# Attention and a feed-forward layer in one kernel: the first batch and the first feed-forward tile put in a written order on all engines

## The chip, the cores and the metric

The kernel runs on one core of a Trainium2 chip. The metric is the time of one execution on the device in microseconds. Before the change it is 1029.81 us, the median of three runs (1029.01 to 1031.52).

## What is computed

For 8 batches of 576 tokens and 8 heads of 64, two attentions in a row, and then a mixing and a feed-forward layer (512 wide, 2048 inside). From the reference, cut:

```python
p_packed = sm_attn(p, k, v)            # 32 packed queries per head
out = sm_attn(q, p_packed, p_packed)   # 576 queries on the 32 packed rows
...
X = np.fft.fft(np.fft.fft(x, axis=1), axis=2)
u = x + np.real(X)
un = (u - mu) / np.sqrt(var + 1e-06)   # mean and variance of each token's 512
ch = np.maximum(un @ w_ch1, 0.0) @ w_ch2
return u + ch
```

## The kernel before

Two kinds of work alternate. `front(b)` (line 241) makes the rows `u` of one batch: attention, the spectrum over tokens and features as products with tables of sines and cosines, the sum with the input and each row's statistics. `ffn` (line 628) takes a tile of 512 rows, four blocks of 128, through the feed-forward layer: 16 rounds of `up` (12 products into `ph`, one PSUM buffer) and `down` (12 products into four accumulators `acc`). There are 8 batches and 9 tiles; a batch gives four blocks, and two batches share one block for the remaining tokens. While `ffn` of tile t runs, `front(t + 1)` is carried on in pieces, one at each of the 31 half rounds (`step`, line 735). "Settled" tiles, 1 to 6, are those with a whole `front` beside them and no weights to load.

All products are made of float32 values split in two parts of fewer bits, the high part by a cast on ACT and the low part by a subtraction on DVE or POOL (`split`, line 98): `hh` and `hl` of the hidden layer, `uh` and `ul` of the rows, `wr_h` and `wr_l` of the weights (`wsplits`, line 618, low part on POOL). The next `up` writes `ph`, and so waits until `hh` (ACT, line 653) and `hl` (DVE, line 654) have read it.

The weights come as 64-bit numbers, 32 pieces of 512 KB. A piece goes by a DMA on SP's queue to a staging place (`fetch`, line 158), ACT takes the high words (`Prelu`, line 179), and DVE shifts them and puts the low bits in (lines 180 and 181). This is done during the first batch and tile 0. The first six pieces are staged in parts of the weight tiles that are filled last (`STG0`), the others in three rotating buffers: one in `ubuf`, two named `wst`.

In `front`, the parts are named by letters in `ORDER` (line 39): s scores, t their transposes, p the packed rows (`packed`, with `bd`, `bdh`, `bdl` for their block diagonal), d the parts of these, q the query scores, g the spectrum of the packed rows (`gh`, `gl`), e, m and a the second softmax in three stages (lines 376 to 428), f, r and h the folding of the weights over tokens (`eo`, `f`, `xl`, `ol`, `fh`, `fl`). 0 and 1 are the two head groups; capitals S, X and U do both groups together; y is a place where the next half round may start. Then follow the products `py`, `pz` and `px`, and `u`. The tables of `py` to `px` are loaded as float32 and split on ACT and DVE (`load_base`, `load_tables`). Between the engines, DVE and POOL share the elementwise work by small tables (`EN`, `EF`, `ES`).

What sets the order: from tile 1 on PE, DVE, ACT and POOL run their instructions as the program writes them (`manual_schedule`, line 748). The first batch and tile 0, with batch 1's `front` beside it, are ordered by the framework's scheduler, which may take a later instruction first; batch 0 and batch 1 have `ORDER` rows of their own. SP's queue always issues in its own order.

Of the kernel before, what the change touches and what calls it, by code (L numbers as in the profile page):

```python
# [16 lines left out]
P = 128  # L17
S = 576
HS = S // 2
D = 64  # L20
# [11 lines left out]
ES = (1, 0, 0)  # L32
# [14 lines left out]
STG0 = [-2, -2, -4, -4, -6, -6]  # L47
STG1 = [9, None, None]
LEAD = 2
# [28 lines left out]
def tile_kernel(ctx, tc, kpT, qT, v, w1, w2, tabC, tabS, tabR, tabB, tabT, sel, ident_d, out):  # L78
# [45 lines left out]
    def load_base():  # L124
        nc.sync.dma_start(sels, sel)
        st = load(tabB, [P, 2, N2], "st_base", "wst")
        h = work.tile([P, 2, N2], F32R, tag="tmp", name="base_h", bufs=3)
        nc.scalar.copy(h, st)
        nc.vector.scalar_tensor_tensor(basis, h.bitcast(F32), selC, st, ALU.mult, ALU.add)
        nc.sync.dma_start(turn, tabT)  # L130

    def load_tables():
        for t, d in enumerate((tabC, tabS)):
            st = load(d, [P, 1, KT], "st_tab", (t, 2))
            split(tbh[t], tbl[t], st[:, 0, :])
        st = work.tile([P, 2, 320], F32, tag="wst", name="st_tabr", bufs=2)
        nc.sync.dma_start(st[:101], tabR)
        for t in range(2):

            h = work.tile([P, DM], F32R, tag="tmp", name="tabr_h", bufs=3)  # L140
            nc.scalar.copy(h[:101, :320], st[:101, t, :])
            nc.vector.scalar_tensor_tensor(
                tbr[t][:101], h[:101, :320].bitcast(F32), selA[:101], st[:101, t, :], ALU.mult, ALU.add)

    sels = cpool.tile([P, 3], F32, name="sels")
    selA, selB, selC = (sels[:, i:i + 1] for i in range(3))
# [9 lines left out]
    def fetch(j, n):  # L158
        i = stages.pop(0)
        if i is None:  # L160
            st = work.tile([P, 512, 2], I32, tag="wst", name="wst", bufs=2)
        elif i < 0:
            st = spot(n, i, [P, 512, 2]).bitcast(I32)
# [3 lines left out]
        fetched[j, n] = st  # L167

    def load_weights(j):

        for n, dst in enumerate((w1f, w2f)):
            if (j, n) not in fetched:
                fetch(j, n)
            st = fetched.pop((j, n))
            low, high = st[:, :, 0], st[:, :, 1]
            c = dst[:, j, :].bitcast(I32)


            nc.scalar.activation(c.bitcast(F32), high.bitcast(F32), AF.Prelu, scale=REBIAS, alpha=-2.0 ** 32)  # L179
            nc.vector.tensor_scalar(c, c, 3, None, ALU.logical_shift_left)  # L180
            nc.vector.scalar_tensor_tensor(c, low, 29, c, ALU.logical_shift_right, ALU.bitwise_or)  # L181
# [59 lines left out]
    def front(b):  # L241
# [31 lines left out]
        def scores(*gs):  # L273
# [9 lines left out]
            tails = now["acc"][2:] if len(gs) == 2 else {gs[0]: bank("s1t")}  # L283
# [146 lines left out]
        def folded(g):  # L430

            a = as_[g]
            eo = work.tile([P, 2, 288], F32, tag="att", name="eo", bufs=ATT)
# [11 lines left out]
        def folded_rest(g):  # L445
# [5 lines left out]
            sm = (nc.vector, nc.gpsimd)[ES[min(b, 2)]]  # L451
# [22 lines left out]
        def folded_parts(g):  # L474
# [236 lines left out]
    gen0 = front(0)  # L711
    for at in gen0:
        if at == "rest":
            break
    cur = Turned(tiles[0][1])
    for i in range(4):
        cur.less(i)
        for move in cur.moves(i):
            move()
        cur.parts(i)  # L720
    for _ in gen0:
        pass
    spare.clear()
    rest = iter(())
    for j in range(ORDER[0].count("D"), LEAD):
        load_weights(j)
    ready, splits = [], wsplits()
    next(splits)
    next(splits)
    for t, (first, tk) in enumerate(tiles):  # L730

        gen = front(t + 1) if t + 1 < B else iter(())
        ended = []

        def step(i):

            next_step()
            if t > 0 and i in (0, 2):
                next(rest, None)
            elif not ended and next(gen, None) == "rest":  # L740
                ended.append(gen)
            if t == 0 and i % 2 == 0 and i // 2 + LEAD < NJ:
                load_weights(i // 2 + LEAD)
            assert i < 2 * NJ - 1 or t + 1 >= B or ended

        nxt = Turned(tiles[t + 1][1]) if t + 1 < len(tiles) else None

        with tc.manual_schedule(engines=MANUAL) if t > 0 else nullcontext():
            ffn(first, cur, step, nxt, t + 1 >= B)
        cur, rest = nxt, gen  # L750


def _tables():
# [31 lines left out]
    sel = np.zeros((P, 3))  # L785
    sel[66:99, 0] = -1.0
    sel[33:66, 1] = sel[100, 1] = -1.0
    sel[D:, 2] = -1.0
    f = np.float32
    return tabs[0].astype(f), tabs[1].astype(f), tabR.astype(f), tabB.astype(f), tabT.astype(f), sel.astype(f), np.eye(P, dtype=f)  # L790


def _prepare(q, k, v, p, moe_w_ch1, moe_w_ch2):
# [19 lines left out]
    for n, t in zip(("tabC", "tabS", "tabR", "tabB", "tabT", "sel", "ident_d"), _tables()):  # L813
        arrays[n] = t
# [37 lines left out]
```

## Time and profile before

| | |
|---|---|
| median of three runs | 1029.81 us |
| the profiled execution: time, span | 1027.14 us, 1025.3 us |
| mean granted TensorE clock | 0.983 |
| PE busy | 978.5 us (95%) |
| DVE busy | 608.8 us (59%) |
| POOL busy | 463.1 us (45%) |
| ACT busy | 425.0 us (41%) |
| read and written in HBM | 48.24 MB and 9.44 MB |

The time is the device's, the span that of the engines' instructions in the profile. Lines in brackets behind an instruction of the timeline say how long its engine was idle before it, and what ended that. `x12` counts instructions; the narrow products of the attention (lines 269 and 326) count twice there. In the waits, three numbers follow: microseconds in total, times, the longest.

### The profile page before, as it was taken

The numbers are of one execution on the slowest core, as the hardware profiler recorded it, in microseconds if no ns is written. First come the engines' busy times: TensorE is split into PE (matmuls) and PEld (weight loads), VectorE is DVE, ScalarE is ACT, GpSimd is POOL, SyncE is SP. The second block draws the span as 40 slices with busy tenths as digits, with TensorE's granted clock in tenths as the row PEclk, the third lists the DMA queues.
The fourth block names the chain that finished last, engine by engine and source line by source line (L and its number), as shares of the span: only waits on it lengthen the run. The fifth ranks groups of instructions, "written<-read, shape, count | busy, mean of one in ns | idle before, by whom it ended". The sixth has DMA issues, their size and how long they took to land.

```text
span 1025.3 us, 14876 instructions
## 1 busy us (share of the span) xinstructions
PE 978.5 (95%) x5692; PEld 795.6 (78%) x5692; DVE 608.8 (59%) x1264; ACT 425.0 (41%) x883; POOL 463.1 (45%) x419
## 2 busy tenths in 40 slices
PE   6489889999999999999999999999999999999998
PEld 2367668878877888788887887788778888887886
DVE  3897994559465856677556846594658562114112
ACT  2556454444443434444444435444435343333322
POOL 1535635364335534454345533643355344444443
PEclk9699899999999999999999999999999999999999
DMA  8328440220023000310041002200210000001001
GB/s 329 109 64 280 157 123 1 93 96 1 1 78 111 1 1 34 108 48 1 1 140 49 1 1 93 96 0 1 82 58 0 1 26 17 0 1 43 1 1 42
DMA packets 17742, 58.64 MB, mean 57 GB/s; under 512 B 2081, under 2 KB 2465, under 8 KB 17670
## 3 DMA queue, kind: packets, MB, share of 16 engines
q1 hardware_dynamic: 17670, 57.68, 16.4%
q8 instruction: 45, 0.74, 0.3%
q14 instruction: 27, 0.22, 0.1%
HBM read 48.24 MB, written 9.44 MB: 56 GB/s over the span
## 4 chain that ended last, share of the span: by engine, by line
PE 76%; DVE 11%; ACT 5%; DMA 3%; issue 2%; POOL 2%; ACTq 0%; SPq 0%; DVEq 0%; POOLq 0%
PE ph L647 35%; PE acc L664 30%; DVE ubuf L567 2%; DMA wst<-w 2%; DVE turned L419 1%; ACT hh L653 1%; PE po L326 1%; PE s L269 1%; ACT junk L217 1%; DVE turned L415 1%; POOL wr_l L100 1%; PE e1tp L303 1%; DVE hl L654 1%; ACT wr_h L99 1%; DVE w2f L181 1%
## 5 line engine op out<-in xcount | busy, mean ns | idle before, releaser
L100 POOL TENSOR_TENSOR wr_l<-w1f,wr_h 128x512 fp32r<-128x512 f32 x144 | 190.8, 1325 | 398.9 <-ACT wr_h L99 395.1
L654 DVE SCALAR_TENSOR_TENSOR hl<-ph,hh 128x512 fp32r<-128x512 f32 x144 | 98.8, 686 | 305.3 <-ACT hh L653 305.0
L647 PE MATMUL ph<-uh,wr_h 128*128 128x512 f32 (+1 forms) x580 | 231.5, 399 | 11.8 <-DVE hl L654 9.6
L100 POOL TENSOR_TENSOR wr_l<-w2f,wr_h 128x512 fp32r<-128x512 f32 x144 | 192.4, 1336 | 91.9 <-ACT wr_h L99 91.9
L664 PE MATMUL acc<-wr_l,hh 128*128 128x512 f32 x576 | 227.0, 394 | 3.0 <-POOL wr_l L100 3.0
L647 PE MATMUL ph<-uh,wr_l 128*128 128x512 f32 (+1 forms) x580 | 229.3, 395 | 0.4 <-POOL wr_l L100 0.4
L647 PE MATMUL ph<-ul,wr_h 128*128 128x512 f32 (+1 forms) x580 | 229.3, 395 | 0.2 <-DVE ul L100 0.2
L664 PE MATMUL acc<-wr_h,hh 128*128 128x512 f32 x576 | 227.8, 396 | 0.0
L664 PE MATMUL acc<-wr_h,hl 128*128 128x512 f32 x576 | 226.2, 393 | 0.0
L653 ACT ACTIVATE hh<-ph 128x512 fp32r<-128x512 f32 x144 | 85.8, 596 | 285.6 <-PE ph L647 285.4
L647 PEld LDWEIGHTS ph<-uh,wr_h 128*128 128x128 f32 x580 | 109.9, 190 | 44.9 <-DVE hl L654 9.8
L647 PEld LDWEIGHTS ph<-uh,wr_l 128*128 128x128 f32 x580 | 110.0, 190 | 24.7 <-POOL wr_l L100 0.8
L664 PEld LDWEIGHTS acc<-wr_l,hh 128*128 128x128 f32 x576 | 108.2, 188 | 26.8 <-POOL wr_l L100 5.4
L647 PEld LDWEIGHTS ph<-ul,wr_h 128*128 128x128 f32 x580 | 110.0, 190 | 23.9 <-issue 1.7
L664 PEld LDWEIGHTS acc<-wr_h,hh 128*128 128x128 f32 x576 | 108.2, 188 | 23.5 <-ACT w2f L179 0.8
L664 PEld LDWEIGHTS acc<-wr_h,hl 128*128 128x128 f32 x576 | 108.2, 188 | 23.1
L99 ACT CAST wr_h<-w2f 128x512 fp32r<-128x512 f32 x144 | 89.4, 621 | 9.4 <-PE ph L647 7.8
L99 ACT CAST wr_h<-w1f 128x512 fp32r<-128x512 f32 x144 | 88.4, 614 | 8.0 <-PE ph L647 3.1
L217 ACT ACTIVATE junk<-ubuf,stat 128x512 f32<-128x512 f32 x36 | 25.8, 718 | 77.3 <-DVE stat L213 77.3
L608 PE MATMUL untp<-ident,un 128*128 128x128 f32 x144 | 37.2, 273 | 1.9 <-DVE stat L220 1.7
L100 POOL TENSOR_TENSOR gl<-turned,gh 128x516 fp32r<-128x516 f32 x16 | 25.2, 1573 | 22.1 <-ACT gh L99 22.1
L567 DVE SCALAR_TENSOR_TENSOR ubuf<-qe,pe 128x512 f32<-128x512 f32 x32 | 34.6, 1115 | 0.5
(199 smaller groups left out, 1292.8 us busy)
## 6 DMA issues: line engine op xcount, KB each, us to landing
kp<-kpT SPq DMA_DIRECT2D x16, 608.0 KB, 4.9
out<-ubuf SPq DMA_DIRECT2D x36, 256.0 KB, 2.1
vt<-v SPq DMA_DIRECT2D x14, 640.0 KB, 4.7
wst<-w SPq DMA_DIRECT2D x17, 512.0 KB, 4.0
qt<-qT SPq DMA_DIRECT2D x14, 576.0 KB, 4.8
ubuf<-w SPq DMA_DIRECT2D x9, 512.0 KB, 4.6
w1f<-w SPq DMA_DIRECT2D x3, 512.0 KB, 11.1
w2f<-w SPq DMA_DIRECT2D x3, 512.0 KB, 11.2
```

The lines of the kernel that those rows point to most:

```text
L99: nc.scalar.copy(hi, src)
L100: (lo_eng or nc.vector).tensor_tensor(lo, src, hi.bitcast(F32), ALU.subtract)
L181: nc.vector.scalar_tensor_tensor(c, low, 29, c, ALU.logical_shift_right, ALU.bitwise_or)
L217: nc.scalar.activation(junk, u, AF.Square, bias=st[:, 1:2], scale=-1.0, accum_out=st[:, 2:3])
L269: nc.tensor.matmul(res[g][c][at, :w.stop - w.start], lhs(g, h), rhs(g, h, w), start=True, stop=True, tile_position=(r, h * NPK))
L303: nc.tensor.transpose(tp[g][:, c * P:(c + 1) * P], e1s[g][:, c * P:(c + 1) * P], ident)
L567: nc.vector.scalar_tensor_tensor(u_of[key], qe, sign, pe, ALU.mult, ALU.add, accum_out=stat_of[key][:, 0:1])
L608: nc.tensor.transpose(tp[:, c * P:(c + 1) * P], un[:, c * P:(c + 1) * P], ident)
L647: nc.tensor.matmul(ph[:, t], l[:, c * P:(c + 1) * P], r[:, c, t], start=(k == 0), stop=(k == 11))
L653: nc.scalar.activation(hh[:, :T], ph[:, :T], AF.Relu)
L654: nc.vector.scalar_tensor_tensor(hl[:, :T], ph[:, :T], 0.0, hh[:, :T].bitcast(F32), ALU.max, ALU.subtract)
L664: nc.tensor.matmul(acc[i], l[:, w], r, start=(j == 0 and k == 0), stop=(j == NJ - 1 and k == 2))
```

## The change

- All of it now runs under `manual_schedule`: `begin` writes the first batch's order, and `step` tile 0's. `ORDER` has two rows: batch 0's, and the one that batches 2 and later had, which is now batch 1's too. So both groups go together through scores, transposes and queries.
- In the first batch, blocks 0 and 1 are made, transposed and given to PE ahead of the products of blocks 2 and 3, and the remainder block moves into half rounds 0 and 2 of tile 0. The mean square deviations of the first four blocks (`squares`, `deviation`) are made in tile 0, two half rounds apart.
- The weight pieces have one list (`wparts`) and are worked off singly: at half round i, piece i + 5 is fetched, piece i + 3 is taken up on ACT, and after the piece of `front` it is shifted on DVE. Nine pieces (W0 to W8) are fetched in the first batch's row of `ORDER`, where four were.
- The host splits the tables into their two parts. The kernel loads the parts with seven DMAs on POOL's queue, and the casts and subtractions of the tables are gone.
- `folded_rest` of batch 0 goes from POOL to DVE (`ES`), and its `eo` lies in a free part of the weight tiles.

Also named with the change: "no idle products". Neither kernel's text has products under such a name.

```diff
-ES = (1, 0, 0)
+ES = ((0, 0), (0, 0), (0, 0))
-ORDER = ("K0 I0 K1 B0 V0 V1 Q0 Q1 W0 W1 W2 W3 s0 t0 p0 d0 s1 t1 p1 q0 e0 d1 g0 q1 e1 m0 m1 a0 f0 r0 h0 a1 "
-         "f1 r1 h1 g1 T0",
-         "s0 s1 y y t0 y t1 y p0 y y y d0 p1 y q0 d1 y y g0 y g1 y e0 q1 e1 y m0 y m1 y a0 a1 y f0 r0 h0 y "
-         "y f1 r1 h1",
+ORDER = ("K0 K1 I0 V0 V1 Q0 Q1 B0 W0 W1 W2 W3 W4 W5 W6 W7 W8 S X p0 p1 d0 d1 L0 U e0 e1 g0 g1 A0 A1 m0 m1 "
+         "a0 a1 f0 r0 f1 r1 h0 h1",
-STG0 = [-2, -2, -4, -4, -6, -6]
+STG0 = [(n, i) for i in (-2, -4, -6) for n in (0, 1)]
-LEAD = 2
+LEAD = 3
...
     def load_tables():
         nc.sync.dma_start(sels, sel)
         for t in range(2):
+            nc.gpsimd.dma_start(tbh[t], tabs[:, t, 0, :])
+            nc.gpsimd.dma_start(tbl[t], tabs[:, t, 1, :])
+            nc.gpsimd.dma_start(tbr[t][:101], tabR[:, t, :])
...
+    wparts = [(0, 0)] + [x for j in range(1, NJ) for x in ((j, 0), (j - 1, 1))] + [(NJ - 1, 1)]
...
+    def load_high(m):
+        if m < len(wparts):
+            j, n = wparts[m]
+            nc.scalar.activation((w1f, w2f)[n][:, j, :], fetched[m][:, :, 1].bitcast(F32), AF.Prelu,
+                                 scale=REBIAS, alpha=-2.0 ** 32)
+    def load_low(m):
+        if m < len(wparts):
+            j, n = wparts[m]
+            c = (w1f, w2f)[n][:, j, :].bitcast(I32)
             nc.vector.tensor_scalar(c, c, 3, None, ALU.logical_shift_left)
+            nc.vector.scalar_tensor_tensor(c, fetched[m][:, :, 0], 29, c, ALU.logical_shift_right, ALU.bitwise_or)
...
-        after(1, squares)
-        after(2, deviation)
+        n = 2 * len(due) if key[0] == 0 else 1
+        after(n, squares)
+        after(n + 1, deviation)
...
+    def begin():
+        rest = front(0)
+        cur = Turned(tiles[0][1])
+        next(rest)
+        load_low(0)
+        next(rest)
+        load_low(1)
+        next(splits)
+        next(rest)
+        steps[0] = 0
+        next(rest)
+        cur.less(0)
+        cur.less(1)
+        next(rest)
+        for move in cur.moves(0) + cur.moves(1):
+            move()
+        load_high(2)
+        next(rest)
+        for k in (2, 3):
+            cur.less(k)
+        for k in (0, 1):
+            cur.parts(k)
+        for move in cur.moves(2) + cur.moves(3):
+            move()
+        for k in (2, 3):
+            cur.parts(k)
+        load_low(2)
+        next(splits)
...
+            def step(i):
+                next_step()
+                if t == 0:
+                    if i + LEAD + 2 not in fetched:
+                        fetch(i + LEAD + 2)
+                    load_high(i + LEAD)
+                if i in (0, 2):
+                    next(rest, None)
+                elif not ended and next(gen, None) == "rest":
+                    ended.append(gen)
+                if t == 0:
+                    load_low(i + LEAD)
```

PE's queue at the start, from the first scores on. `s_` with a number is a group's score bank, `e1tp` and `e1tq` the transposes of its weights, `po` the packed rows. Before:

```order
L269 MATMUL s1t<-kp 32x64 x4
L269 MATMUL s_117<-kp 32x512 x4
L269 MATMUL s1t<-kp 32x64 x4
L306 MATMUL e1tq<-ident,e_131 64x128
L269 MATMUL s_186<-kp 32x512
L303 MATMUL e1tp<-ident,e_131 128x128 x4
L269 MATMUL s_186<-kp 32x512 x3
L306 MATMUL e1tq<-ident,e_200 64x128
L326 MATMUL po<-w1f,e1T 32x64 x20
```

And now, from the last two score products on:

```order
L265 MATMUL s_122<-kp 32x512
L265 MATMUL s_123<-kp 32x512
L299 MATMUL e1tp<-ident,e_145 128x128 x4
L299 MATMUL e1tp<-ident,e_154 128x128 x4
L302 MATMUL e1tq<-ident,e_145 64x128
L302 MATMUL e1tq<-ident,e_154 64x128
L322 MATMUL po<-w1f,e1T 32x64 x20
L322 MATMUL po<-w2f,e1T 32x64 x20
```

The second group's scores have moved from behind the first group's transposes to a place among the first group's scores.

POOL's queue in the first batch: `bd` and `bdl` of both groups, then `s_` with a number, the second softmax of group 1. Before:

```order
L334 TENSOR_TENSOR bd<-pp_169,bmask 128x256
L100 TENSOR_TENSOR bdl<-bd,bdh 128x256
L334 TENSOR_TENSOR bd<-pp_238,bmask 128x256
L100 TENSOR_TENSOR bdl<-bd,bdh 128x256
L100 TENSOR_TENSOR gl<-turned,gh 128x516
L381 TENSOR_TENSOR s_298<-s_298,m_301 128x576
L397 TENSOR_TENSOR s_298<-s_298,d_314 128x576
L455 TENSOR_TENSOR f<-a 128x3 x2
```

And now:

```order
L98 TENSOR_TENSOR bdl<-bd,bdh 128x256
L129 DMA tbh_87<-tabs 128x448
L130 DMA tbl_89<-tabs 128x448
L131 DMA tbr_93<-tabR 101x320
L129 DMA tbh_88<-tabs 128x448
L130 DMA tbl_90<-tabs 128x448
L131 DMA tbr_94<-tabR 101x320
L377 TENSOR_TENSOR s_285<-s_285,m_295 128x576
L98 TENSOR_TENSOR gl<-turned,gh 128x516 x2
```

Six table loads stand ahead of group 1's subtraction, both `gl` stand behind it, and the steps of `f` are gone from here.

DVE's queue in the middle of tile 0, up to an `hl`. `w1f` and `w2f` are the weights, `turned` the spectrum of the packed rows, `s_` with a number the query scores of a group. Before:

```order
L180 TENSOR_SCALAR w2f<-w2f 128x512
L419 TENSOR_TENSOR turned<-turned 128x258 x2
L415 TENSOR_TENSOR turned<-pg,turn 128x516 x2
L396 RECIPROCAL z_1207<-z_1207 128x18
L419 TENSOR_TENSOR turned<-turned 128x258 x2
L181 SCALAR_TENSOR_TENSOR w2f<-wst,w2f 128x512
L180 TENSOR_SCALAR w1f<-w1f 128x512
L180 TENSOR_SCALAR w2f<-w2f 128x512
L374 STREAM_TRANSPOSE s_1171<-s2Tt 128x64
L427 STREAM_TRANSPOSE a<-s_1021 128x576
L654 SCALAR_TENSOR_TENSOR hl<-ph,hh 128x512
```

And now, from one `hl` to the next:

```order
L650 SCALAR_TENSOR_TENSOR hl<-ph,hh 128x512
L411 TENSOR_TENSOR turned<-pg,turn 128x516 x2
L415 TENSOR_TENSOR turned<-turned 128x258 x2
L175 TENSOR_SCALAR w1f<-w1f 128x512
L176 SCALAR_TENSOR_TENSOR w1f<-ubuf,w1f 128x512
L370 STREAM_TRANSPOSE s_1011<-s2Tt 128x64
L370 STREAM_TRANSPOSE s_1010<-s2Tt 128x64
L370 STREAM_TRANSPOSE s_1011<-s2T 128x512
L370 STREAM_TRANSPOSE s_1010<-s2T 128x512
L175 TENSOR_SCALAR w2f<-w2f 128x512
L176 SCALAR_TENSOR_TENSOR w2f<-wst,w2f 128x512
L650 SCALAR_TENSOR_TENSOR hl<-ph,hh 128x512
```

A weight's two steps now stand together, one weight and one piece of `front` in each half round, and weights of other rounds no longer stand ahead of `hl`.

More of the change, by code (lines that the diff above doesn't have):

```diff
@@ L77, in tile_kernel @@
 @with_exitstack
-def tile_kernel(ctx, tc, kpT, qT, v, w1, w2, tabC, tabS, tabR, tabB, tabT, sel, ident_d, out):
+def tile_kernel(ctx, tc, kpT, qT, v, w1, w2, tabs, tabR, tabB, tabT, sel, ident_d, out):
     nc = tc.nc
@@ L124, in load_base @@
     def load_base():
[L125 to L129, printed above, removed]
+        nc.gpsimd.dma_start(basis, tabB)
         nc.sync.dma_start(turn, tabT)
     def load_tables():
[L133 to L137, printed above, removed]
-        for t in range(2):
[L140 to L148, printed above, removed]
+        nc.sync.dma_start(sels, sel)
+        for t in range(2):
+            nc.gpsimd.dma_start(tbh[t], tabs[:, t, 0, :])
+            nc.gpsimd.dma_start(tbl[t], tabs[:, t, 1, :])
+            nc.gpsimd.dma_start(tbr[t][:101], tabR[:, t, :])
+    sels = cpool.tile([P, 1], F32, name="sels")
+    selB = sels[:, 0:1]
     fetched = {}
@@ L166, in fetch @@
         nc.sync.dma_start(st, (w1, w2)[n][:, j, :].bitcast(I32).rearrange("p (n t) -> p n t", t=2))
[L167 to L179, printed above, removed]
+        fetched[m] = st
+    def load_high(m):
[5 more added lines that the diff above has]
+        if m < len(wparts):
+            j, n = wparts[m]
+            c = (w1f, w2f)[n][:, j, :].bitcast(I32)
             nc.vector.tensor_scalar(c, c, 3, None, ALU.logical_shift_left)
-            nc.vector.scalar_tensor_tensor(c, low, 29, c, ALU.logical_shift_right, ALU.bitwise_or)
+            nc.vector.scalar_tensor_tensor(c, fetched[m][:, :, 0], 29, c, ALU.logical_shift_right, ALU.bitwise_or)
     u_of, stat_of, place_of, free = {}, {}, {}, list(range(NU))
@@ L280, in keys_of @@
                 return kps[g][side(g, h):side(g, h) + D, h // 2, w]
-            tails = now["acc"][2:] if len(gs) == 2 else {gs[0]: bank("s1t")}
+            tails = now["acc"][2:] if b > 0 else {g: bank("s1t") for g in gs}
             sc = narrow(gs, lambda g, h: keys_of(g, h, slice(S, S + NPK)), keys_of, "s1", tails)
@@ L432, in folded @@
             a = as_[g]
-            eo = work.tile([P, 2, 288], F32, tag="att", name="eo", bufs=ATT)
+            eo = work.tile([P, 2, 288], F32, tag="att", name="eo", bufs=ATT) if b else spot(g, 2, [P, 2, 288])
             f = work.tile([P, FW], F32, tag="att", name="f", bufs=ATT)
@@ L709, in tile_kernel @@
     tiles = [(i, keys[i:i + 4]) for i in range(0, len(keys), 4)]
[L711 to L718, printed above, removed]
-            move()
[L720 to L748, printed above, removed]
+    ready, splits = [], wsplits()
@@ new lines, in begin @@
+    def begin():
[13 more added lines that the diff above has]
+        for move in cur.moves(0) + cur.moves(1):
+            move()
+        load_high(2)
[10 more added lines that the diff above has]
+        next(splits)
+        spare.clear()
+        return cur, rest
@@ new lines, in tile_kernel @@
+    with tc.manual_schedule(engines=MANUAL):
+        cur, rest = begin()
+        for t, (first, tk) in enumerate(tiles):
+            gen = front(t + 1) if t + 1 < B else iter(())
+            ended = []
+            def step(i):
[10 more added lines that the diff above has]
+                    load_low(i + LEAD)
+                assert i < 2 * NJ - 1 or t + 1 >= B or ended
+            nxt = Turned(tiles[t + 1][1]) if t + 1 < len(tiles) else None
@@ L749, in tile_kernel @@
             ffn(first, cur, step, nxt, t + 1 >= B)
-        cur, rest = nxt, gen
+            cur, rest = nxt, gen
 def _tables():
@@ L812, in _prepare @@
     }
-    for n, t in zip(("tabC", "tabS", "tabR", "tabB", "tabT", "sel", "ident_d"), _tables()):
+    for n, t in zip(("tabs", "tabR", "tabB", "tabT", "sel", "ident_d"), _tables()):
         arrays[n] = t
```

34 lines of the change are left out of this document (21 added, 13 removed).

## The prediction

> **What bounds the kernel now.** I read the page's slices first, then busy time by stage, then who PE waits for in the slow stage, then the queue of the engine it waits for. The slices (each digit a tenth of a slice of 25.6 us):
>
> ```profile
> PE   6489889999999999999999999999999999999998
> PEclk9699899999999999999999999999999999999999
> ```
>
> Only the first six or seven slices are short of full. By stage (length, then busy us and count of PE, weight loads, DVE, ACT, POOL, then granted clock, DMA share, GB/s):
>
> ```profile
> 0.00:20.80 20.80, 12.81 (x126) 5.75 (x127) 5.30 (x18) 5.78 (x15) 2.23 (x12) 1.00 0.91 345
> 20.80:45.50 24.70, 8.46 (x60) 5.93 (x59) 21.33 (x47) 11.37 (x22) 13.92 (x33) 0.66 0.45 146
> 45.50:49.60 4.10, 3.92 (x19) 3.62 (x19) 4.10 (x7) 2.41 (x7) 1.10 (x1) 0.53 0.07 7
> 49.60:62.70 13.10, 11.18 (x102) 9.28 (x100) 12.70 (x37) 9.05 (x24) 3.41 (x5) 1.00 0.20 52
> 62.70:187.20 124.50, 113.01 (x624) 88.52 (x623) 96.13 (x196) 60.68 (x121) 62.68 (x53) 0.95 0.39 127
> 297.40:406.30 108.90, 108.07 (x662) 88.96 (x661) 70.97 (x151) 46.39 (x98) 49.61 (x43) 1.00 0.13 45
> ```
>
> The last row is a settled tile: PE busy 108.07 of 108.9 us, so PE is the bound. Tile 0 runs from its first `ph` product to its first output step (the next two rows) and takes 124.5 us; before it lie 62.7 us of first batch, where DVE, not PE, is full (21.33 of 24.7, 12.70 of 13.1).
>
> ```profile
> 62.70 0.36 PE L647 MATMUL ph<-uh,wr_h 128*128 128x256 f32 x1
> 187.22 0.74 DVE L700 SCALAR_TENSOR_TENSOR ubuf<-acc,stat,ubuf 128x512 f32<-128x512 f32 x1
> ```
>
> PE's waits in tile 0, the two long ones in its timeline, and DVE's queue before the first of these:
>
> ```profile
> PE ph L647 <- DVE hl L654: 9.6, 3, 4.4
> ```
> ```profile
> 116.15 0.79 PE L647 MATMUL ph<-uh,wr_h 128*128 128x512 f32 x1 [4.40 <-DVE hl L654]
> 133.34 0.50 PE L647 MATMUL ph<-uh,wr_h 128*128 128x512 f32 x1 [3.74 <-DVE hl L654]
> ```
> ```profile
> 110.24 1.65 DVE L181 SCALAR_TENSOR_TENSOR w2f<-wst,w2f 128x512 int32<-128x512 int32 x1
> 111.81 1.49 DVE L180 TENSOR_SCALAR w1f<-w1f 128x512 int32<-128x512 int32 x1
> 115.45 0.64 DVE L654 SCALAR_TENSOR_TENSOR hl<-ph,hh 128x512 fp32r<-128x512 f32 x1
> ```
>
> `ph` has one buffer, so the next `up` cannot start until `hl` has read it. Here `hl` stands behind weight steps of other rounds; PE waits 4.40 us and comes back slow (0.79 us for a product). DVE has 96.13 us of work in 124.5, so it could keep up: the fault is bunching, not amount.
>
> **Tile 0, the large term.** Over 108.9 us, 16 rounds, a round has 6.8 us of PE and 96.13/16 = 6.0 us of DVE. The new order gives each half round one weight's shift-and-or, one piece of the next batch, and `hl` directly behind its `up`. PE's work becomes that of a settled tile, 108.9, which already holds the remainder block that now moves in behind the first batch. What stalls remain has no row. One end: a settled tile's, under 1 us. The other: those of now, 124.5 - 113.01 = 11.5 idle and 113.01 - 108.07 = 4.9 of slow clock. I take 3.6, a quarter way up, nearer the settled tile since its queues are written the same way, but DVE there is 71 busy and here 96 of 109. Tile 0: 112.5, a gain of **12.0** (bounds 15.6 and 0).
>
> The weights must keep up too. Three buffers rotate after the first nine, so one use of a buffer may take three half rounds, 10.2 us. A use, from the chain of waits:
>
> ```profile
> 78.42 4.81 DMA wst<-w
> 83.25 0.68 ACT w2f L179
> 83.95 0.68 DVE w2f L180
> 84.65 0.70 DVE w2f L181
> ```
>
> 4.81 + 0.68 + 0.68 + 0.70 = 6.9 us: 3.3 to spare. In SP's queue the loads of batch 1's values, queries and next keys now stand among them and wait for PE; each wait ends within the half round that issues it, so the spare covers it. Without it see the third rival.
>
> **The first batch.** Scores of both head groups now alternate on PE and need both keys first.
>
> ```profile
> 4.95 1.93 PE L269 MATMUL s<-kp 64*32 64x512 f32 x8
> 11.69 1.93 PE L269 MATMUL s<-kp 64*32 64x512 f32 x6
> 22.50 1.04 PE L269 MATMUL s2T<-w2f,ppT 64*32 64x512 f32 x8
> ```
> ```profile
> 193.72 0.86 PE s L269 x16
> ```
> ```profile
> kp<-kpT SPq DMA_DIRECT2D x16, 608.0 KB, 4.9
> ```
>
> The first group's wide products now start at 4.95, and the second's end at 13.6. The second keys land 608 KB / 345 GB/s = 1.8 us after the first, so that they start near 6.8; alternated, 16 products take 0.86 us where one group alone takes 1.04, so both together take one group's slow 1.93: done at 8.7, 4.9 us earlier. About 1.9 is given back (0.61 + 0.74 + 0.41, and a hop): on ACT the cast of the packed keys now stands behind both diagonals, which adds a `bd`, a `bdl` and a cast:
>
> ```profile
> 20.57 0.61 POOL L334 TENSOR_TENSOR bd<-pp,bmask 128x256 f32<-128x256 f32 x1 [0.89 <-DVE pp L331]
> 21.70 0.74 POOL L100 TENSOR_TENSOR bdl<-bd,bdh 128x256 fp32r<-128x256 f32 x1 [0.52 <-ACT bdh L99]
> 21.22 0.41 ACT L99 CAST bdh<-bd 128x256 fp32r<-128x256 f32 x1 [2.18 <-POOL bd L334]
> ```
>
> Query scores end at 20.5 instead of 23.5 (22.50 + 1.04): **3.0** gained.
>
> From there to the end of `fl` DVE is full in both kernels. It takes over the second and first group's small folding steps from POOL:
>
> ```profile
> 137.06 0.54 DVE L455 TENSOR_TENSOR f<-eo 128x45 f32<-128x45 f32 x4
> 138.00 0.41 DVE L481 SCALAR_TENSOR_TENSOR xl<-eo,xh 128x256 fp32r<-128x256 f32 x1
> 36.20 1.37 DVE L483 TENSOR_TENSOR ol<-eo,oh 128x256 fp32r<-128x256 f32 x1
> ```
> ```profile
> DVE fl L485 <- ACT fh L479: 2.8, 2, 1.5
> ```
> ```profile
> 26.83 1.28 POOL L100 TENSOR_TENSOR gl<-turned,gh 128x516 fp32r<-128x516 f32 x1 [4.39 <-ACT gh L99]
> 28.07 1.16 POOL L381 TENSOR_TENSOR s<-s,m 128x576 f32<-128x576 f32 x1
> 36.10 1.19 POOL L425 TENSOR_TENSOR s<-s,z 128x576 f32<-128x576 f32 x1
> ```
>
> A group's set takes 138.00 - 137.06 = 0.94 us, two 1.9. Back comes about 1 us of DVE held while POOL works (`ol` took 1.37 beside POOL's 1.19 at 36.10; the 0.41 of `xl`, as large, is its free time), and the 2.8 us that `fl` waited for `fh`, behind POOL's folding. A wait is added: DVE's transpose of group 1's weights stands ahead of group 0's folding, and waits for POOL, which now has both `gl` ahead of group 1's last steps, 1.3 more; behind it stand all folding steps, and then PE.
>
> POOL has six table loads between `bdl` and group 1's subtraction. No POOL-issued load is in this trace. One end is a load that costs POOL nothing; the other a POOL step of 1.19, six 7.1. I take the latter, since POOL itself must issue them: `bdl` now ends near 19.4 (22.4 less 3.0), the loads at 26.5, and the subtraction could have begun at 28.07 - 3.0 = 25.1. That costs 1.4. Sum of this stage: 1.9 - 1.0 - 2.8 + 1.3 + 1.4 = **+0.8**.
>
> The Trainium skill (SBUF — State Buffer, § SBUF: two separate sides) speaks against this part: while DVE runs a two-port step, POOL cannot write the descriptors of a load that it issues; a later section there has 620 ns grow to 3100. By that the 1.4 would be 5 or more, and the sum that of rival 1. The rows above show such an exclusion between computing steps only.
>
> Then `py`: about 31 of its 36 products now come after `fl`. From a gap PE comes back at half clock, 19 products in 4.1 us (0.215 each) in the third stage above, and has the full clock some 4 us later:
>
> ```profile
> 45.04 0.58 PE L237 MATMUL py<-gh,fh 128*128 128x258 f32 x1 [1.11 <-ACT gh L99]
> ```
>
> So 19 products take 4.1 us and 12 more 1.4: 5.5 where 4.1 stood, **+1.4**. From there to the first `ph`:
>
> ```profile
> 54.07 1.79 DVE L567 SCALAR_TENSOR_TENSOR ubuf<-qe,pe 128x512 f32<-128x512 f32 x1
> 61.10 0.68 DVE L581 TENSOR_TENSOR xa<-px,spec 64x512 f32<-64x512 f32 x1
> ```
>
> DVE's 12.70 of 13.1 us loses the remainder block (0.68, and its two half-wide steps, 1.3 in all), the first `w2f` weight (0.68 + 0.70) and such holds as that of 1.79; against that, the second pair's products stand behind the first pair's transposes on PE, some 2 us that DVE waits. 13.1 becomes 11 to 13; I take 12.0, **-1.1**. The table splits taken off ACT and DVE lay beside PE's `py` and gain nothing; their cover is gone with nothing behind it. The first nine weight loads, 4.7 MB, have landed by 28 us at 345 GB/s, even behind as much again; they are wanted after 45.
>
> First batch: -3.0 + 0.8 + 1.4 - 1.1 = **-1.9** (bounds -6, without the give-backs, and +3, with POOL's loads held).
>
> **The sum.** Against the profiled execution's span, 1025.3 (its time was 1027.1): -12.0 - 1.9 = -13.9, 1011.4. The median of the runs, 1029.8, lies 4.5 above that span: **1015.9**. Tiles 1 to 8 keep their code and order: nothing there.
>
> **Rivals.** (1) POOL's loads are held up. If each of the six waits for a DVE step of 0.7 as well, they take 11.3 us, end at 30.7, and group 1 is 5.6 late in place of 1.4: 1020. For: the 1.37 us `ol`. Chance 0.12.
> (2) DVE bounds tile 0. It idles 124.5 - 96.1 = 28.4 us there now, of this
>
> ```profile
> DVE hl L654 <- ACT hh L653: 12.5, 8, 4.7
> ```
>
> If in order it keeps the other 15.9 and half of these, tile 0 is 96.1 + 15.9 + 6.2 = 118.2: 1022. With all of them it is what it is now: 1028. For: 0.8 us of room a round. Against: waiting for `hh` means that DVE is early. Chance 0.15.
> (3) Slower: the weights come late.
>
> ```profile
> w1f<-w SPq DMA_DIRECT2D x3, 512.0 KB, 11.1
> ```
>
> In order, ACT's and DVE's weight steps hold up `hh` and `hl` behind them. It decides above a landing of 10.2 - 2.1 = 8.1 us. At 11.1, as in the crowded start, a buffer's use takes 13.2, a weight 4.4 in place of 3.4, 23 weights 23 us more: 1015.9 + 23 - 3.6 (the stalls already counted) = 1035. For: SP's queue holds batch 1's loads among them. Against: the load above took 4.81. Chance 0.08.
> (4) The order changes little, because PE is still let go late in each round by something unseen: within 3 us of now. Chance 0.06. "No idle products" names nothing that I find in the diff, and is given no price.
>
> **How the numbers follow.** The main case has 0.59: 1015.9, between 1008 (tile 0 without stalls, first batch 3 better) and 1022 (twice the stalls, first batch 3 worse). Rival 1 and most of rival 2 lie within 1025. Leaving out rivals 3 and 4 and the worst of 2: 1007 to 1025. A change under 0.3%, 3 us, can't be told from none by such a measurement. Faster 0.85 (main, 1 and 2), same 0.06 (rival 4), slower 0.09 (rival 3 and a little that I don't see).
>
> **What would show it.** Right: first `ph` near 61; first output step near 173, 112 to 113 us later; few `ph`<-`hl` waits; tiles after it 108.9 apart. Wrong: DVE or ACT waiting for weight loads in tile 0 (rival 3), POOL busy with table loads past 26 and group 1's subtraction behind them (rival 1), DVE without idle time in tile 0 and PE waiting for `hl` in many rounds (rival 2).

## The result, and the profile after

| | before | after |
|---|---|---|
| median of four runs each | 1029.41 us | 1037.65 us |
| ratio, with its 95% interval | | 1.0078 (1.0059 to 1.0097) |
| span of the profiled execution | 1025.3 us | 1035.9 us |
| first `ph` product | 62.70 | 64.24 |
| first output step (end of tile 0) | 187.22 | 187.17 |
| a settled tile | 108.9 | 110.2 |

The kernel became 8 us slower where 14 us faster was forecast. First the slices of the page after:

```profile
PE   4379889999999999999999999999999999999998
PEclk8599999999999999999999999999999999999999
```

They look like those of before: short at the start, full from tile 1 on. The busy time by stage says more (columns as in the prediction: length, busy time and count of PE, weight loads, DVE, ACT, POOL, then granted clock, DMA share, GB/s):

```profile
0.00:20.80 20.80, 10.22 (x156) 5.00 (x156) 5.22 (x21) 5.94 (x16) 6.05 (x18) 0.94 0.94 362
20.80:45.50 24.70, 3.98 (x20) 3.01 (x13) 23.80 (x65) 8.09 (x14) 9.60 (x10) 0.50 0.49 171
45.50:51.00 5.50, 5.46 (x33) 5.46 (x34) 2.62 (x6) 1.88 (x5) 0.00 (x0) 0.69 0.00 0
51.00:64.20 13.20, 7.77 (x57) 7.12 (x56) 11.39 (x29) 4.37 (x10) 1.41 (x1) 0.94 0.00 1
64.20:187.20 123.00, 114.07 (x673) 90.77 (x672) 105.18 (x203) 66.83 (x138) 61.96 (x56) 0.98 0.41 129
297.30:407.50 110.20, 109.53 (x662) 88.93 (x661) 71.17 (x151) 46.44 (x98) 49.23 (x43) 1.00 0.13 44
```

The last row is a settled tile. It has the same 662 products as before, at the same granted clock of 1.00, and no more idle time (0.67 us; 0.83 before), but 109.53 us of busy PE where 108.07 stood. The bounds of tile 0, from the timeline:

```profile
64.24 0.56 PE L643 MATMUL ph<-uh,wr_h 128*128 128x256 f32 x1
187.17 2.72 DVE L696 SCALAR_TENSOR_TENSOR ubuf<-acc,stat,ubuf 128x512 f32<-128x512 f32 x4
```

Tile 0 took 122.9 us (124.5 before), and the first batch 1.5 more, so both kernels end tile 0 at 187.2. From there to the end are 1035.9 - 187.17 = 848.7 us; before it was 838.1. The whole loss of 10.6 us on the span lies in tiles 1 to 8, whose code and order the change leaves alone.

The chain that ended last shows why, most clearly in the last tile but one, where no further batch runs beside the products: start, length, and how many follow each other. Before, and after:

```profile
874.70 2.72 PE ph L647 x12
877.42 2.72 PE acc L664 x12
880.14 2.72 PE ph L647 x12
```

```profile
873.54 2.80 PE acc L660 x12
876.34 2.76 PE ph L643 x12
879.10 2.80 PE acc L660 x12
881.90 2.76 PE ph L643 x12
```

Twelve 512-wide products take 2.72 us before, and 2.80 (`down`, into `acc`) or 2.76 (`up`, into `ph`) after. One group follows the other without a gap, and no other engine is waited for.

### The profile page after: what moved, and what is told of

It is laid out like the page before. It is cut to its first block, busy times and chain, and to the rows that moved or that the text cites. A ratio compares the mean times of both kernels' runs of the same rounds, so it can differ in the third digit from the quotient of the medians.

```text
span 1035.9 us, 14872 instructions
## 1 busy us (share of the span) xinstructions
PE 981.7 (95%) x5692; PEld 793.2 (77%) x5692; DVE 618.4 (60%) x1283; ACT 422.6 (41%) x878; POOL 457.4 (44%) x402
## 4 chain that ended last, share of the span: by engine, by line
PE 79%; DVE 11%; ACT 4%; issue 3%; POOL 2%; DMA 0%; SPq 0%; ACTq 0%; DVEq 0%; POOLq 0%
PE ph L643 35%; PE acc L660 31%; DVE ubuf L563 2%; DVE turned L415 1%; POOL wr_l L98 1%; ACT hh L649 1%; PE po L322 1%; ACT junk L212 1%; DVE turned L411 1%; PE s L265 1%; PE py L235 1%; PE e1tp L299 1%; PE py L233 1%; PE py L234 1%; DVE un L597 1%
## 5 line engine op out<-in xcount | busy, mean ns | idle before, releaser
L98 POOL TENSOR_TENSOR wr_l<-w1f,wr_h 128x512 fp32r<-128x512 f32 x144 | 187.2, 1300 | 434.5 <-ACT wr_h L97 431.0
L660 PE MATMUL acc<-wr_l,hh 128*128 128x512 f32 x576 | 230.0, 399 | 3.0 <-POOL wr_l L98 3.0
L660 PE MATMUL acc<-wr_h,hl 128*128 128x512 f32 x576 | 228.9, 397 | 0.0
L233 PE MATMUL py<-gh,fh 128*128 128x258 f32 x64 | 19.0, 297 | 18.6 <-ACT fh L475 18.6
```

The costliest lines, as they stand in the source:

```text
L98: (lo_eng or nc.vector).tensor_tensor(lo, src, hi.bitcast(F32), ALU.subtract)
L233: nc.tensor.matmul(o, lh, rh, start=first, stop=False)
L660: nc.tensor.matmul(acc[i], l[:, w], r, start=(j == 0 and k == 0), stop=(j == NJ - 1 and k == 2))
```

## Experiments: where the settled tiles lose 1.3 us

The instructions being the same, their operands' places in SBUF were compared. The work pool, from which the kernel takes its tiles, lays out its tags in the order of their first use, and the new program order uses `wr`, the split weights, ahead of `spec`, `un`, `uh` and `ul`. By the compiled programs, `wr` lies at byte 206720 of a partition before and at 184128 after, `uh` at 190336 and 202624, while `hh` and `hl` stay at 219008 and 223104. Of a product's two operands, the stationary one is what its weight load reads, and the moving one is what the product itself reads. `up` reads `uh` or `ul` as the moving operand and has `wr` as the stationary one; `down` reads `wr` as the moving one and has `hh` or `hl` as the stationary one. Four kernels put the tiles elsewhere and change nothing else:

```
e1   before the first use of wr:  tiles of the tags spec0, spec1, ln, uh, ul   (never used)
e2   before the first use of wr:  work.tile([P, 16], F32, tag="pad0", bufs=1)
     and behind it:               work.tile([P, 16], F32, tag="pad1", bufs=1)
e3   the same two in the kernel before
e4   as e2, without pad1
```

> The changed kernel with the tags of the work pool laid out as in the kernel before (the two spec tiles, un, uh, ul, then the six wr tiles at 206720 and on); instructions and their order unchanged. Theory A (the settled tiles are 1.3 us longer because of where the tiles lie in SBUF): twelve 512-wide products take 2.72 us again, settled tiles 108.9, time 1026 to 1028. Rival B (something else in the changed order, such as the front's products or their banks): settled tiles stay at 110.2, time 1037.

> The changed kernel with 64 bytes left free ahead of the six wr tiles and 64 behind them: they start at 184192, a multiple of 128, in place of 184128, which is not; all that follows moves by 128. Theory A1 (what counts is that wr starts at a multiple of 128 bytes): settled tiles 108.9, time 1026 to 1028. Theory A2 (what counts is the region that wr lies in, 184128 on instead of 206720 on): 110.2, 1037. Rival B: 110.2, 1037.

> The kernel before with 64 bytes left free ahead of the wr tiles and 64 behind: they start at 206784, which is 64 past a multiple of 128. Theory A1: settled tiles go from 108.9 to 110.2, time from 1029.4 to 1038 to 1040. Theory A2 and rival B: 108.9, 1029.

> The changed kernel with 64 bytes free ahead of the wr tiles and none behind: wr starts at a multiple of 128, and un, uh, ul, hh and hl now start 64 past one. By theory A1, if the alignment of the moving operand counts, up's products (moving uh and ul) go to 2.80 for twelve and down's (moving wr) to 2.72; if that of the stationary operand counts, the other way round, since hh and hl are down's stationary ones and wr up's. Settled tiles 109.6 by either, time about 1032. Theory A2 and rival B: 110.2, 1037.

e1 gave 1028.75 us, 1.0002 of before (0.9992 to 1.0012). From its first output step to its end are 1027.3 - 189.35 = 838.0 us, and before it was 838.1: the places alone make the 10.6 us, and rival B falls. But e2 did not help: 1041.80 (1.0135, 1.0119 to 1.0152), more than any theory had. e3 made the kernel before as slow, 1043.14 (1.0152, 1.0137 to 1.0167), and e4 came to 1038.38 (1.0104, 1.0090 to 1.0119). So neither a multiple of 128 for `wr` (A1) nor one operand's own alignment is what counts. From the same stretch of e2's chain, where each of these operands starts at a multiple of 128:

```profile
872.31 2.78 PE ph L643 x12
875.10 2.78 PE acc L660 x12
```

Take the remainder of each start, what is left of its byte when it is divided by 256. In e2 `wr` has the remainder 128, and `uh`, `ul`, `hh` and `hl` have 0. That left two theories: only equal remainders are good (C), or only a region or certain absolute places are (D, which holds A2). Two more kernels leave `wr` where the change put it, in the slow region and off a multiple of 128, and move what follows it:

```
e5   behind the first use of wr:  work.tile([P, 112], F32, tag="pad", bufs=1)     448 bytes
e6   behind the first use of wr:  work.tile([P, 48], F32, tag="pad", bufs=1)      192 bytes
```

> The changed kernel with 448 bytes left free behind the six wr tiles, nothing else: wr stays at 184128, and un, uh, ul, hh and hl now have the same remainder by 512 as wr, 320 (before the change all had 384; in the changed kernel wr has 320 and the others 384). Theory C (what counts is that the operand that a product reads and the one that its weight load reads start at the same place within 512 or 256 bytes): twelve 512-wide products take 2.72 us, settled tiles 108.9, time 1028 to 1029. Theory D (an absolute place counts: the region, or a multiple of 128): settled tiles 110 or more, time 1037 or more.

> The changed kernel with 192 bytes left free behind the wr tiles: un, uh, ul, hh and hl lie 256 bytes from wr by the remainder of 512. Theory C with a period of 256: 2.72 us for twelve products, 1028 to 1029. Theory C with a period of 512: 2.76 to 2.80, 1036 to 1042. Theory D: as it was, 1037.

Both are as fast as the kernel before: 1027.83 (0.9996, 0.9985 to 1.0006) and 1027.62 (0.9990, 0.9981 to 0.9999). D falls. By 512 the starts are equal in e5 and 256 apart in e6, and both are fast, so the period is 256 bytes. A settled tile of e5, and its chain:

```profile
296.10:405.00 108.90, 108.04 (x662) 88.86 (x661) 70.73 (x150) 46.43 (x98) 49.18 (x43) 1.00 0.13 45
```

```profile
442.64 2.72 PE acc L660 x12
445.36 2.72 PE ph L643 x12
448.08 2.72 PE acc L660 x12
```

The table has the remainders by 256 and what twelve products take, in us, where no batch runs beside them:

| kernel | `wr` | `uh`, `ul` | `hh`, `hl` | `up` | `down` | time |
|---|---|---|---|---|---|---|
| before | 128 | 128 | 128 | 2.72 | 2.72 | 1029.41 |
| e1 | 128 | 128 | 128 | 2.72 | 2.72 | 1028.75 |
| e5 | 64 | 64 | 64 | 2.72 | 2.72 | 1027.83 |
| e6 | 64 | 64 | 64 | 2.72 | 2.72 | 1027.62 |
| after | 64 | 128 | 128 | 2.76 | 2.80 | 1037.65 |
| e4 | 128 | 192 | 192 | 2.76, 2.79 | 2.80 | 1038.38 |
| e2 | 128 | 0 | 0 | 2.78, 2.80 | 2.78, 2.80 | 1041.80 |
| e3 | 192 | 128 | 0 | 2.79 | 2.80 | 1043.14 |

A product takes 2.72 / 12 = 0.227 us when the moving operand and the stationary one start at the same place within 256 bytes (seen at the remainders 64 and 128), and 0.230 to 0.233 otherwise. Moving less stationary, 64 gives 2.76 to 2.79, 128 gives 2.78 to 2.80 and 192 gives 2.79 to 2.80. This is shown for 512-wide fp32r products with 128-wide weights that follow each other; why it is so no run shows. The other experiments stand on e1 or e5, the changed kernel with equal remainders.

## Experiments: why tile 0 did not become shorter

With the places mended the kernel is as fast as before, not 14 us faster. Tile 0 still takes 122.7 us in e1 and e5. PE's waits in it, after the change:

```profile
PE ph L643 <- ACT wr_h L97: 5.9, 3, 2.3
PE ph L643 <- DVE s L370: 1.3, 1, 1.3
PE ph L643 <- DVE hl L650: 1.0, 1, 1.0
PE acc L660 <- POOL wr_l L98: 0.7, 2, 0.4
```

The waits for `hl` are gone as forecast (9.6 us before, 1.0 now). In their place PE waits for `wr_h`, which ACT makes from a weight that DVE has yet to finish. The middle of tile 0:

```profile
102.60:156.20 53.60, 46.41 (x199) 36.07 (x198) 51.06 (x94) 27.78 (x53) 30.55 (x26) 0.97 0.48 142
```

DVE is busy for 51.06 of 53.6 us there. The first experiment leaves out DVE's two steps for each weight of tile 0, on e1:

```diff
-                if t == 0:
-                    load_low(i + LEAD)
```

> The changed kernel with the old places, and without DVE's two steps (shift, and shift and or) for each weight that is loaded in tile 0: the low words of these weights are left out, so its products are not the reference's. DVE loses 28 weights at 1.3 to 1.7 us, some 40 of its 105 us in tile 0. Theory E (DVE's amount of work bounds the middle of tile 0): first product to first output step goes from 122.7 to 110 to 113 us, time 1016 to 1019. Rival F (the order of ACT's and POOL's queues, or the loads, holds tile 0): 119 or more, time 1025 or more.

Measured: 1017.46 (0.9900, 0.9887 to 0.9914), in the range of theory E. Tile 0, and all that PE still waits for in it:

```profile
64.33:176.97 112.64, 110.64 (x673) 89.86 (x672) 66.56 (x145) 66.38 (x138) 57.77 (x56) 0.99 0.42 141
```

```profile
PE acc L660 <- POOL wr_l L98: 1.6, 2, 1.1
PE ph L643 <- DVE s L370: 0.3, 1, 0.3
```

112.6 us is about the length that the prediction gave tile 0 (112.5) with all of DVE's work in it. So these steps, 105.5 - 66.6 = 39 us of DVE, hold tile 0 by 10 us, and neither the loads nor ACT's or POOL's queues by themselves do (F falls). Without them a weight also goes straight from ACT's step for its high words to ACT's `wr_h`, so t1 alone does not tell DVE's amount of work from the place of these steps ahead of `wr_h`. Next, 5 us of other DVE work go to POOL, on e5:

```diff
-ES = ((0, 0), (0, 0), (0, 0))
+ES = ((0, 0), (1, 1), (0, 0))
```

> The changed kernel with the same phase, and the small folding steps of batch 1, which fall into tile 0, on POOL in place of DVE (both groups: 8 of 0.58 us and 16 shorter ones). Theory E: DVE loses 5 to 6 us in its full stretch, tile 0 goes from 122.7 to 117 to 119 us, time 1023 to 1025. Rival K (POOL's steps hold DVE's by as much as they take off it, or fl waits for fh behind them): 121 to 124 us, time 1027 to 1029.

Measured: 1027.67 (0.9991, 0.9981 to 1.0001), no gain: rival K. Tile 0, and two of DVE's waits in its middle:

```profile
66.44:189.19 122.75, 113.15 (x673) 90.51 (x672) 99.99 (x178) 67.16 (x138) 68.24 (x80) 0.98 0.39 130
```

```profile
DVE hl L650 <- ACT hh L649: 2.7, 1, 2.7
DVE fl L481 <- ACT fh L475: 1.3, 2, 0.7
```

DVE's 105.2 us became 100.0, and tile 0 not shorter by a tenth of a us. PE's wait for `wr_h` is nearly what it was; in e5 it is 6.3, 3, 2.5, and here:

```profile
PE ph L643 <- ACT wr_h L97: 6.1, 3, 2.3
```

The moved steps run at 131 to 147 us in e5, and of PE's waits there only the last one for `wr_h` (2.5 us, up to 145.5) and one of 0.5 come after their start. So g3 could have gained some 3 us, and not the 4 to 6 of theory E. The last wait for `wr_h` is 2.3 now: DVE waits instead, among others for `fh` behind POOL's small steps. g3 says little on whether DVE's amount holds the rest. Then the order, with all work in place. One kernel gives tile 0 back to the scheduler, one makes the weights further ahead:

```
u2   tile 0 outside the manual schedule:
     with tc.manual_schedule(engines=MANUAL) if t > 0 else nullcontext():
v1   LEAD = 6 in place of 3;  for i < 3, load_high(i + 3) and load_low(i + 3) as well
```

> The changed kernel with the same phase, the first batch in program order and tile 0 by the scheduler, as before the change. Theory E (DVE's amount of work bounds tile 0, whatever the order): from first product to first output step 121 to 126 us in place of 122.7, time 1026 to 1031. Rival J (the program order took away waits worth some 10 us and something else gave them back): 130 us or more, 1035 or more.

> The changed kernel with the same phase (1027.8), and in tile 0 each weight is made six half rounds ahead of its use in place of three: the first three half rounds make two weights each. Amount of work unchanged. Theory E (DVE's amount in the full stretch): at most the 3 weights at 1.4 us that move out of the full stretch are gained, tile 0 118.5 to 121 us in place of 122.7, time 1024 to 1026. Theory L (the weights come too shortly ahead of their use, and a little more lead takes all of PE's 10 us of waits away): tile 0 113 to 115, time 1018 to 1020.

u2: 1026.49 (0.9986, 0.9975 to 0.9996); its first output step starts at 185.85, e5's at 187.13. The scheduler's order of tile 0, bunched as it is, costs nothing against the program order. v1 was slower, 1032.66 (1.0039, 1.0028 to 1.0049), which neither theory had; L falls. Its tile 0, and what PE waits for:

```profile
64.22:191.61 127.39, 115.05 (x673) 91.93 (x672) 105.09 (x203) 66.68 (x138) 60.36 (x56) 0.96 0.36 125
```

```profile
PE ph L643 <- DVE hl L650: 7.8, 4, 3.4
PE acc L660 <- POOL wr_l L98: 2.5, 3, 1.7
```

DVE's work is the same 105.1 us. The waits for `wr_h` are gone, and those for `hl` are back at 7.8. So a longer lead does not shorten the tile. But ACT waits 4.0 us for loads in v1 (1.1 in the changed kernel), and how much of v1's loss is theirs is not shown. The last one keeps the lead and puts a weight's two steps ahead of the piece of batch 1, on the kernel u1 below (first output step at 183.47):

```diff
                     load_high(i + LEAD)
+                    load_low(i + LEAD)
                 if i in (0, 2):
...
-                if t == 0:
-                    load_low(i + LEAD)
```

> The first batch by the scheduler (1022.7, first output step at 183.5), tile 0 in program order, and in each half round DVE's two steps for a weight ahead of the piece of batch 1 in place of behind it. Theory E (DVE's amount): PE's waits for wr_h turn into waits for hl or s, first output step within 2 us of 183.5, time 1021 to 1025. Theory Q (the place in DVE's queue): the 6 us of waits for wr_h go, first output step at 178 to 180, time 1017 to 1019.

Measured: 1039.54 (1.0113, 1.0094 to 1.0132), 16.8 us more than u1 and outside of both theories. DVE's waits in the middle of its tile 0:

```profile
DVE w2f L175 <- ACT w2f L167: 6.6, 4, 2.0
DVE hl L650 <- ACT hh L649: 5.2, 2, 4.9
DVE w1f L175 <- ACT w1f L167: 3.7, 4, 2.7
```

DVE now waits 10.3 us for the high words that ACT has just been given, a time that the piece of batch 1 used to fill. So the weights' steps on DVE hold tile 0 by 10 us, as t1 shows. Every order tried with them in place (the changed one, the scheduler's, v1 and x3) only chose which wait shows, or added one. That it is DVE's amount of work, whatever its order, is argued from this and from DVE being full in the middle; whether another order of the same work would come near 112 us stays open.

## Experiments: the first batch

Query scores end early, as forecast (DVE's transposes start on them), and `fl` ends where it did, at 45.49:

```profile
21.07 1.31 DVE L370 STREAM_TRANSPOSE s<-s2T 128x512 f32<-128x512 f32 x2 [1.33 <-PE s2T L265]
44.54 0.95 DVE L481 TENSOR_TENSOR fl<-f,fh 128x776 fp32r<-128x776 f32 x1
```

That stretch, before and after:

```profile
23.54:45.46 21.92, 5.68 (x24) 4.88 (x25) 18.94 (x43) 10.12 (x19) 12.75 (x31) 0.62 0.42 142
```

```profile
21.04:45.50 24.46, 3.74 (x13) 2.84 (x13) 23.80 (x65) 8.09 (x14) 9.36 (x9) 0.50 0.48 169
```

DVE is busy 4.9 us more and idle 2.3 less. Part of that is work that lay ahead of this stretch. In the kernel before, two of the spectrum's four products ran before the query scores had ended; after the change all four come behind them, 1.4 us more:

```profile
20.84 0.70 DVE L415 TENSOR_TENSOR turned<-pg,turn 128x516 f32<-128x516 f32 x1 [0.35 <-PE pg L411]
22.23 0.68 DVE L415 TENSOR_TENSOR turned<-pg,turn 128x516 f32<-128x516 f32 x1
```

Another part is the folding steps of both groups, taken over from POOL, so they were given back, on e1:

```diff
-ES = ((0, 0), (0, 0), (0, 0))
+ES = ((1, 1), (0, 0), (0, 0))
```

> The changed kernel with the old places, and the small folding steps of the first batch's two head groups on POOL in place of DVE (the second group's were there before the change too). Theory G (DVE's amount bounds the first batch from the query scores to the end of fl): that stretch goes from 24.5 to 22.5 us, time 1026 to 1027. Rival H (fl then waits for fh behind POOL, as it did before the change): 24.5 to 26.5, time 1028.7 to 1031.

Measured: 1029.07 (1.0007, 0.9995 to 1.0019), and `fl` starts 1.6 us later than in e1 (44.56):

```profile
46.16 0.97 DVE L481 TENSOR_TENSOR fl<-f,fh 128x776 fp32r<-128x776 f32 x1 [1.29 <-ACT fh L475]
```

Theory G's gain of 2 us did not come, and `fl` waits for `fh` as rival H had it. But e1's own 1028.75 also lies in rival H's range, so that this part of the change gains 1.6 us at `fl` is seen in the profile, and a gain in time is not shown. Then the first batch was given back to the scheduler, with tile 0 left in program order, on e5:

```diff
-    with tc.manual_schedule(engines=MANUAL):
-        cur, rest = begin()
+    cur, rest = begin()
+    with tc.manual_schedule(engines=MANUAL):
```

> The changed kernel with the same phase (448 bytes left free behind the wr tiles, time 1027.8), and the first batch ordered by the scheduler again; tile 0 and all after it in program order. Theory G (DVE's amount bounds the first batch after the query scores): fl ends within 1 us of 45.6 and the first ph product starts at 63 to 65.5, time 1027 to 1029. Rival I (program order itself costs the first batch the time that earlier query scores gained): fl ends at 43, first ph product at 61.5, time 1025.

Measured: 1022.74, 0.9947 of before (0.9932 to 0.9962), the one version here that clearly beats both kernels. `fl` ends at 45.16, as G said, and not at 43, as rival I said; the gain comes behind it, and is more than either theory had. From the end of `fl` to the end of `py`, in u1 and in e5:

```profile
45.16:47.80 2.64, 2.64 (x23) 2.64 (x23) 2.63 (x7) 1.77 (x6) 0.00 (x0) 0.96 0.00 0
```

```profile
45.61:51.20 5.59, 5.53 (x33) 5.54 (x34) 2.69 (x8) 1.88 (x5) 0.00 (x0) 0.68 0.00 0
```

The scheduler has products that need no `fl` ahead of it, so that 23 are left in place of 33, and the clock in that stretch is 0.96 against 0.68. Its first `up` product starts at 55.80, on the first pair of blocks alone, and its first output step at 183.47, 3.7 earlier than e5's. Two of the reasons were then tried in program order, each alone, and three together:

```
w1   batch 0: gh*fh and gl*fh of all six py tiles first, then gh*fl of each
h1   "... h0 h1 D0" in ORDER[0];  load_low(1) where load_low(0) stood
y1   w1, h1, and next(rest) for px of blocks 2, 3 ahead of cur.moves(0) + cur.moves(1)
```

> The changed kernel with the same phase, and in the first batch the 24 products of py that need no fl written ahead of the 12 that do. Theory M (program order holds these behind fl, at half clock; the scheduler had them ahead): py ends 2 to 3 us earlier, first ph product at 61.5 to 62.5 in place of 64.4, time 1025 to 1026. Rival N (the scheduler's gain lies in what follows py): no change, 1027.8.

> The changed kernel with the same phase, and DVE's steps for the first two weights one place earlier: the first right behind fl, where DVE waits for py, the second where the first stood. In the changed kernel the second stands ahead of the first pe, which starts 1.1 us after spec is there. Theory: first ph product 1.0 us earlier, 63.3 in place of 64.4, time 1026.8. Rival (the chain behind it waits for PE's half clock anyway): no change, 1027.8.

> The changed kernel with the same phase (1027.8, first ph product at 64.4), all in program order; py's products that need no fl ahead of those that do, DVE's steps for the first two weights one place earlier, and the second pair's px products ahead of the first pair's transposes. Theory O (the scheduler's 4 to 5 us are these three, each hidden behind the others): first ph product at 60 to 61.5, since px no longer waits for the transposes (2.2 to 2.6 us of DVE's waits) nor pe for a weight (1.5), time 1023 to 1025. Rival P (the gain comes from the first up product starting on the first pair of blocks alone, which only the scheduler does): 63 or later, 1027 or more.

w1: 1029.01 (1.0006, 0.9993 to 1.0020); h1: 1028.20 (1.0002, 0.9993 to 1.0012). Neither gains. Single profiles of this stretch differ by as much as such steps are worth: with the first batch's instructions and their order unchanged, the first `ph` product starts at 64.2 in the changed kernel, 64.4 in e5 and 66.6 in e1. One reason is that PE's first products behind `fl` take 0.42 us each for 3.4 us in e5 and for 5.3 in e1, and 0.28 from then on. In w1 `py` ends at 49.8, 1.4 earlier than in e5, but the first `ph` product starts at 65.05, within that spread: DVE's weight steps still stand ahead of `pe`, and the second pair's `px` still behind the first pair's transposes, which wait for `un`. With all three, y1 reaches it at 61.42, in theory O's 60 to 61.5:

```profile
56.98 1.06 PE L619 MATMUL untp<-ident,un 128*128 128x128 f32 x8 [0.53 <-DVE un L612]
60.55 1.11 PE L619 MATMUL untp<-ident,un 128*128 128x128 f32 x8 [2.51 <-DVE un L612]
61.42 0.36 PE L658 MATMUL ph<-uh,wr_h 128*128 128x256 f32 x1
```

But its tile 0 then takes 125.05 us, ends at 186.47, and the time is 1026.34 (0.9978, 0.9967 to 0.9990), 1.5 us less than e5 and not the 1023 to 1025 of theory O: 3.0 us gained, 2.3 of them lost again in tile 0. Last, the longer lead with the scheduler's first batch (x1), and with w1 (x2):

> The first batch by the scheduler (1022.7) and the weights six half rounds ahead. Theory E: 1019 to 1021. Theory L: 1013 to 1015.

> All in program order, with the products of py ahead of fl and the weights six half rounds ahead. Theory E with M: 1021.5 to 1024. Theory L with M: 1015.5 to 1018. The two gains add, since one lies ahead of tile 0 and the other in it.

x1 gave 1028.02 (0.9994, 0.9979 to 1.0010) and x2 1032.94 (1.0044, 1.0031 to 1.0056), slower than either theory had, both with v1's loss of 4 to 5 us.

## Why the prediction was wrong, point by point

- **"Tiles 1 to 8 keep their code and order: nothing there."** This step failed, and with it the sign. Code and order were kept, but the program order of the first batch also sets where the tiles lie. It cost 10.6 us on the span; e5 undoes it with 448 unused bytes of each partition.
- **Tile 0, "a gain of 12.0".** It was 1.6 in the changed kernel and 1.8 in e5. Right that the waits for `hl` would go; wrong in what was left. The stalls, put at 3.6 above a settled tile of 108.9, were 13.8 in e5 (122.7 - 108.9). "The fault is bunching, not amount" failed: the scheduler's bunched order (u2) costs nothing, and t1 shows that DVE's weight steps hold the tile. DVE's 96 us became 105, partly the remainder block's steps that moved in, partly longer steps (a weight's two steps took 1.54 us in the mean, 1.43 before). This comes nearest to rival 2, which had 0.15 and 1022 to 1028, though PE waits for `wr_h` and not for `hl` in many rounds. What spoke against it, that DVE waits for `hh` and so is early, was read from the whole tile. DVE is full in the middle 54 us and less busy at both ends, and so it was in the kernel before, 49.96 of 53.8 us:

```profile
100.90:154.70 53.80, 44.53 (x215) 35.63 (x215) 49.96 (x100) 26.78 (x51) 27.12 (x22) 0.90 0.44 139
```

- **Weights in time.** Right: `wr_h` is late because of DVE, not of a load (ACT waits once for one, 1.1 us), and rival 3 did not happen.
- **Query scores 3.0 earlier.** About 2.5 (21.0 in place of 23.5).
- **Up to `fl`, +0.8.** +2.5. The table loads that were charged at 1.19 each cost about half:

```profile
18.78 0.61 POOL L129 DMA_DIRECT2D tbh<-tabs  x1
21.56 0.55 POOL L131 DMA_DIRECT2D tbr<-tabR  x1
```

  They ended at 22.1 and held up nothing, so rival 1 did not happen, and the 1.4 charged for them was nothing. The wait of 1.3 behind POOL's `gl` was 0.24. Two terms failed the other way. Of the -1.0 for holds, `ol` did go from 1.37 to 0.41, but other steps took longer: group 0's multiplication, a 0.75 us step before, took 1.42. And the 1.4 of the two `turned` products that came in from ahead of the stretch had no term. That `fl` would no longer wait was right, and f1 shows it 1.6 later with the folding on POOL. The Trainium skill (SBUF — State Buffer, § A bandwidth-pool intuition that's wrong (but worth ruling out)) has a POOL-issued load grow from some 620 to some 3100 ns beside a DVE `tensor_copy`. No run here shows that case: DVE's steps beside the six loads were transposes, copies and subtractions that read PSUM, and each load cost POOL 0.54 to 0.61 us.
- **`py` +1.4.** Right: 5.5 us at a clock of 0.69, where 4.1 stood.
- **To the first `ph` product, -1.1.** It was 13.2, as before. The 2 us that DVE waits for `px` behind the transposes, named there, were there (1.6). w1 and h1 each took away another wait and gained nothing, and y1, with these two changes and the second pair's `px` ahead of the first pair's transposes, starts the first `ph` product 3.0 earlier than e5. That the three stand in parallel is argued from this; the one for `px` was not removed alone.
- **The sum.** With the places mended, e5 is at 1027.8: first batch +1.7 and tile 0 -1.8 in its profile, so that nothing is left of the gain either. The first batch by the scheduler (u1) is worth 5 us more than the changed one.

## What to carry to other kernels

When the order of first use changes, compare the addresses of the operands of the hot products before and after, and compare the time of a dozen of them in a stretch that the change leaves alone; a few unused bytes in a pool can be worth more than the change. Before counting on an engine that is 77% busy over a tile, look at its share in each third of it. Before moving its steps to another engine, see whether the waits that you want gone come after them. Of several waits that stand in parallel, price the last one that remains and not the one removed.

## What the hardware showed that was not expected

Two operands of a product that differ in their start within 256 bytes cost 3.3 to 6.7 ns for each 512-wide product (2.76 and 2.80 us for twelve, against 2.72), 1% of this kernel, without any wait in the trace. The Trainium skill (SBUF — State Buffer, § Who interferes with whom) says that PE never waits on anyone, and has its reads of the moving operand and of the weights as two independent ports. The measurement differs from what one would take from that: e1 to e6 change only where these tiles and a few beside them lie, and the products' time changes. Whether PE's two reads meet each other, or the other engines' writes of the same tiles, is not shown.

A POOL-issued load cost POOL 0.54 to 0.61 us, six of them 3.3 us in all, with DVE at work for part of it.
